# Retention queries scaled on GpSimd instead of retention outputs on VectorE, with a deeper input pipeline

## The chip, the cores and the metric

The kernel runs on one core of a Trainium2 chip. The metric is the time on the device in microseconds (us), lower is better. The engines are named as in the profile: PE is TensorE's matmul side and PEld its weight loads, DVE is VectorE, ACT is ScalarE, POOL is GpSimd, SP is the engine that issues most DMAs. 

## What is computed

Three layers, all float32, one after the other on 2304 tokens (4 batches of 576) of width 512:

```python
def _attn_ref(q, k, v):                      # q, k, v: (4, 8, 576, 64)
    scores = scale * np.matmul(q, k.transpose(0, 1, 3, 2))
    gamma = 1.0 - 2.0 ** (-5.0 - np.arange(H, dtype=np.float32))
    rel = pos[:, None] - pos[None, :]
    Dmat = np.where(rel >= 0, gamma[:, None, None] ** rel[None, :, :], 0.0)
    return np.matmul(scores * Dmat, v)       # retention
# rms norm, then (silu(x @ w_gate) * (x @ w_val)) @ w_out, d_ff = 1536
# then 8 experts: relu(x @ w1[e]) @ w2[e], weighted by a Sinkhorn-normed router
```

Only the retention layer and the first weights of the gated layer are touched by the change.

## The kernel before

The work has three stages: retention with the norm sums (about the first 87 us), the gated layer (five blocks of tokens times six sweeps over the weights), and the experts, which take most of the time. The order of the instructions on each engine is the order in which the code is written (a manual schedule); an engine runs its own list in that order, and the lists wait for each other by semaphores.

Retention runs over 16 pairs of heads, i = 0 to 15: batch b = i // 4, pair pr = i % 4, two heads in one 128-partition tile. The 576 positions are four chunks of 128 and a tail of 64. For a pair:

- `load_pair` (L279) brings kT and qT (feature by position, 128x576), ks (position by feature, 128x512) and vs (128x576); kT and ks have two buffers each, qT and vs three.
- `scale_keys` (L289) multiplies ks by a decay on ACT (L295).
- `scores` (L297): 8 matmuls of kT and qT into `sc` in PSUM (L310) and two for the tail (L313), then DVE multiplies by a mask into `am` (L314). The masks are made at the start on POOL from a causal table and the decays g_in (L460).
- `states` (L320): 8 small matmuls of ks and vs (L331), a scan over the chunks on DVE (L334) and the tail mask `mt` (L335).
- `outputs` (L338): matmuls of the states with qT for the tail (L347, L349) and the chunks (L352), then of `am` with vs (L361). DVE scales the results by the decays `g_out` while it moves them from PSUM into `acc`: the tail in L357 (128x64), the chunks in L366 (128x512). ACT squares them (L371) and, for pr > 0, POOL adds the squares to those of the batch so far (L373).

The loop at L473 writes, for pair i: the loads of pair i+2 (qT, vs) and one weight tile, `scores(i + 1)`, the first part of `outputs(i)`, `states(i + 1)`, the second part of `outputs(i)`, the loads of pair i+3 (kT, ks), `scale_keys(i + 2)`, one call of `step_weights`, and the last part of `outputs(i)`. In places it also runs the norm: `norm_sums` (L389) of batch 0, 1 and 2 starts at i = 5, 9 and 13 with five matmuls into `ss` (L398), then DVE, a power on POOL (L405) and more DVE; `norm` (L412) of batch 0 runs from i = 7, that of batch 1 from i = 13; each of the two has matmuls into `rb` (L421).

`step_weights` (L161) takes each weight tile that is being narrowed one step on. A tile of 64-bit weights (128x1024 words) becomes a float32 pair high and low in steps that go back and forth: ACT abs (L134); DVE three instructions (L136 to L138); ACT abs (L140); DVE sign (L142), which frees the raw tile; ACT cast to the high part (L156); DVE subtraction for the low part (L158). Two tiles are under way at most.

Of the kernel before, what the change touches and what calls it, by code (L numbers as in the profile page):

```python
# [9 lines left out]
F32 = mybir.dt.float32  # L10
# [7 lines left out]
B, H, S, D = 4, 8, 576, 64  # L18
NP = H // 2
# [6 lines left out]
C = 128  # L26
# [32 lines left out]
def retention_glu_experts(ctx: ExitStack, tc: tile.TileContext, a, out):  # L59
# [22 lines left out]
    const.tile([128, 40], F32, name="spacer_w")  # L82
# [183 lines left out]
    tables = tabs.tile([128, 2 * H + 2 * NP + C + TAIL], F32, name="tables")  # L266
    at, views = 0, []
    for size in (H, H, NP, NP, C, TAIL):
        views.append(tables[:, at:at + size])
        at += size  # L270
    g_in, g_key, g_step, g_tail, causal, causal_t = views
    steps = acc_d[:, :, (B - 1) * S:(B - 1) * S + D * NC]
    g_out = tabs.tile([128, NP, C], F32, name="g_out")
    mhalf = nrm.tile([128, NC + 1], F32, name="mhalf")
# [4 lines left out]
    def load_pair(i, *names, queue=nc.sync):  # L279
        if i >= B * NP:  # L280
            return
        b, pr = divmod(i, NP)
        t = {}
        for n in names:
            t[n] = ld.tile([128, a[n].shape[-1]], F32, tag=n, name=f"{n}{i}", bufs=2 if n[0] == "k" else 3)
            queue.dma_start(t[n], a[n][b, pr])
        loaded.setdefault(i, {}).update(t)

    def scale_keys(i):  # L289
        if i >= B * NP:  # L290
            return
        for h in range(2):
            hh = 2 * (i % NP) + h
            ks = loaded[i]["ks"].rearrange("p (c h d) -> p c h d", h=2, d=D)[:, :, h, :]
            nc.scalar.mul(ks, ks, g_key[:, hh:hh + 1])  # L295

# [41 lines left out]
    def outputs(i):  # L338
# [18 lines left out]
        nc.vector.tensor_mul(xf[:, NC * C:], ot, g_out[:, pr, :TAIL])  # L357
        yield
        for c in range(NC):
# [6 lines left out]
        nc.vector.tensor_mul(  # L366
            xf[:, :NC * C].rearrange("p (c i) -> p c i", c=NC), o,
            g_out[:, pr:pr + 1, :].to_broadcast([128, NC, C]),
        )
# [85 lines left out]
    nc.gpsimd.memset(wg[:, KD * E:], 0.0)  # L455
    nc.scalar.dma_start(tables, a["tables"])
    mask_rows = masks.rearrange("p a b c d -> p (a b c) d")
    for pr in range(NP):
        for hh in (2 * pr, 2 * pr + 1):
            nc.gpsimd.tensor_mul(mask_rows[:, hh, :], causal, g_in[:, hh:hh + 1].to_broadcast([128, C]))  # L460
        step = steps[:, pr].rearrange("p (d c) -> p d c", c=NC)[:, :, 1:]
        nc.gpsimd.tensor_copy(step, g_step[:, pr:pr + 1].to_broadcast([128, D, NC - 1]))
    load_pair(0, "kT", "ks")
    load_pair(0, "qT", "vs", queue=nc.scalar)
    load_pair(1, "kT", "qT")
    load_pair(1, "ks", "vs")
    nc.sync.dma_start(g_out.rearrange("p h i -> p (h i)"), a["g_out"])
# [6 lines left out]
    load_pair(2, "kT", "ks")  # L474
    for i in range(B * NP):
        b, pr = divmod(i, NP)
        load_pair(i + 2, "qT", "vs")
        load_weights(1)
# [9 lines left out]
        load_pair(i + 3, "kT", "ks")  # L488
        scale_keys(i + 2)
        step_weights(load=False, apart=1)  # L490
# [896 lines left out]
def _tables():  # L1387
# [16 lines left out]
    t["tables"] = np.concatenate(joined, 1)  # L1404
# [56 lines left out]
```

## Time and profile before

| | |
|---|---|
| median of 3 runs | 1983.78 us (1983.07 to 1984.54) |
| profiled execution | 1984.0 us, its span 1981.7 us |
| PE busy | 1964.9 us, 99% of the span |
| DVE / ACT / POOL busy | 1554.6 / 944.1 / 877.8 us |
| chain that ended last | PE 90%, DVE 5%, DMA 3%, ACT 1% |

The span is the profiled execution from its first to its last instruction; the 2.3 us beside it lie outside the instructions. A busy PE says that matmuls follow each other, not that they run at their peak, so the stretches in which PE waits, and for what, tell more than the busy share.

### The profile page before, as it was taken

What the parts mean: (1) busy time and instruction counts of PE and PEld (TensorE: products, weight loads), DVE (VectorE), ACT (ScalarE), POOL (GpSimd) and SP (SyncE); (2) the same over time, 40 slices, a digit from 0 to 9 for tenths busy, and PEclk for the clock granted to TensorE, in tenths of its full rate; (3) what the DMA queues carried; (4) which work ended last, traced back from release to release, by engine and by line L of the source; (5) the groups of instructions that cost most, each with busy time, mean ns of one, the idle gap of its engine ahead of it and who ended that gap; (6) DMA issues with size and microseconds to landing.
All of it is one profiled execution on the core that took longest, in us unless ns stands there. A gap on an engine that the chain in (4) does not pass through costs nothing.

```text
span 1981.7 us, 31851 instructions
## 1 busy us (share of the span) xinstructions
PE 1964.9 (99%) x11540; PEld 1868.2 (94%) x11540; DVE 1554.6 (78%) x2496; ACT 944.1 (48%) x1902; POOL 877.8 (44%) x817
## 2 busy tenths in 40 slices
PE   9999999999999999999999999999999999999998
PEld 7788888988889989999999999999999999999998
DVE  6868999886678776777787777777787777777777
ACT  4556555544454435444455444444455444444443
POOL 2314344444144424445564445454465454544543
PEclk9999999999999999999999999999999999999999
DMA  8418999988377887667768767677667676666763
GB/s 306 162 57 292 310 325 325 317 300 264 114 291 297 296 305 279 264 254 266 270 237 296 270 241 280 252 261 274 239 260 273 252 279 258 257 262 245 277 256 143
DMA packets 167853, 515.51 MB, mean 260 GB/s; under 512 B 17960, under 2 KB 71984, under 8 KB 150032
## 3 DMA queue, kind: packets, MB, share of 16 engines
q1 hardware_dynamic: 167024, 512.00, 71.2%
q8 instruction: 90, 1.47, 0.3%
q0 software_dynamic: 240, 0.79, 0.1%
q10 hardware_dynamic: 432, 0.70, 0.1%
q14 instruction: 67, 0.55, 0.1%
HBM read 390.40 MB, written 123.02 MB: 259 GB/s over the span
## 4 chain that ended last, share of the span: by engine, by line
PE 90%; DVE 5%; DMA 3%; ACT 1%; issue 1%; SPq 0%; POOL 0%; ACTq 0%; DVEq 0%
PE py L910 10%; PE pz L910 10%; PE px L910 10%; PE qx L1145 9%; PE qy L1145 9%; PE qz L1145 9%; PE qz L910 4%; PE gv L194 4%; PE gv L196 4%; PE gv L195 4%; PE e L1145 2%; PE pv L1145 2%; PE x L195 2%; PE x L196 2%; PE x L194 2%; PE y L195 2%
## 5 line engine op out<-in xcount | busy, mean ns | idle before, releaser
L1327 POOL TENSOR_TENSOR acc<-z,a_block 128x384 f32<-128x384 f32 x83 | 84.3, 1016 | 563.1 <-DVE z L1321 563.1
L699 POOL TENSOR_TENSOR ahead_raw<-ahead_raw 128x256 f32<-128x256 f32 x164 | 150.8, 919 | 211.1 <-DVE wslots L681 71.7
L1139 DVE TENSOR_TENSOR xlo<-acc,xhi 128x384 fp32r<-128x384 f32 x250 | 236.1, 970 | 2.8 <-ACT xhi L1135 2.7
L910 PE MATMUL py<-sx,w1s 128*128 128x384 f32 x1152 | 231.8, 335 | 0.9 <-ACT py L1247 0.6
L910 PEld LDWEIGHTS py<-sx,w1s 128*128 128x128 f32 x1152 | 202.4, 188 | 4.0 <-ACT py L1247 2.6
L1135 ACT CAST xhi<-acc 128x384 fp32r<-128x384 f32 x332 | 162.0, 513 | 91.3 <-POOL acc L1327 46.5
L910 PE MATMUL px<-xhi,w1s 128*128 128x384 f32 x640 | 189.1, 336 | 0.4 <-DVE t L220 0.4
L1156 DVE TENSOR_TENSOR acc<-acc,qz 128x384 f32<-128x384 f32 x246 | 134.8, 548 | 25.2 <-PE qz L1145 25.1
L1174 ACT COPY qz<-qy 128x384 f32<-128x384 f32 x167 | 77.4, 463 | 139.4 <-PE qy L1145 132.1
L1166 ACT COPY qy<-qx 128x384 f32<-128x384 f32 x167 | 77.4, 463 | 123.6 <-PE qx L1145 116.3
L1139 POOL TENSOR_TENSOR xlo<-fifth,xhi 128x384 fp32r<-128x384 f32 x83 | 108.4, 1307 | 38.1 <-ACT xhi L1135 38.1
L1156 DVE TENSOR_TENSOR acc<-acc,qx 128x384 f32<-128x384 f32 x123 | 67.4, 548 | 70.9 <-PE qx L1145 70.9
L910 PEld LDWEIGHTS px<-xhi,w1s 128*128 128x128 f32 x640 | 117.9, 188 | 1.1 <-DVE t L220 0.7
L910 PE MATMUL pz<-sx,w1s 128*128 128x384 f32 x576 | 115.4, 334 | 0.0
L910 PE MATMUL pz<-xhi,w1s 128*128 128x384 f32 x384 | 113.4, 335 | 0.0
L1349 POOL TENSOR_TENSOR fifth<-acc 128x384 f32<-128x384 f32 x83 | 111.2, 1339 | 0.0
L1348 POOL TENSOR_TENSOR acc<-z 128x384 f32<-128x384 f32 x83 | 109.7, 1322 | 0.0
L910 PE MATMUL px<-xlo,w1s 128*128 128x384 f32 x320 | 107.0, 334 | 0.0
L910 PEld LDWEIGHTS pz<-sx,w1s 128*128 128x128 f32 x576 | 101.3, 188 | 0.7
L1135 ACT CAST xhi<-a_block 128x384 fp32r<-128x384 f32 x84 | 43.2, 514 | 121.5 <-DVE a_block L1290 121.5
L1139 DVE TENSOR_TENSOR xlo<-z,xhi 128x384 fp32r<-128x384 f32 x84 | 88.5, 1053 | 0.0
L1329 POOL TENSOR_TENSOR acc<-acc,z 128x384 f32<-128x384 f32 x83 | 85.4, 1029 | 6.5
(409 smaller groups left out, 6085.6 us busy)
## 6 DMA issues: line engine op xcount, KB each, us to landing
w1s<-w_kept SPq DMA_DIRECT2D x85, 1792.0 KB, 7.1
w2s<-w_kept SPq DMA_DIRECT2D x42, 1024.0 KB, 6.9
w_extra<-w_kept SPq DMA_DIRECT2D x42, 768.0 KB, 7.6
w2c<-w_kept SPq DMA_DIRECT2D x42, 512.0 KB, 7.7
w2c<-w_kept SPq DMA_DIRECT2D x84, 256.0 KB, 7.9
ahead_raw<-in_w_dram SPq DMA_DIRECT2D x41, 512.0 KB, 5.4
w_kept<-w1s SPq DMA_DIRECT2D x11, 1792.0 KB, 6.6
w_kept<-wslots SPq DMA_DIRECT2D x74, 256.0 KB, 4.4
```

The costliest lines, as they stand in the source:

```text
L194: nc.tensor.matmul(ps, lhsT=lh, rhs=rh, start=start, stop=False)
L195: nc.tensor.matmul(ps, lhsT=lh, rhs=rl, start=False, stop=False)
L196: nc.tensor.matmul(ps, lhsT=ll, rhs=rh, start=False, stop=stop)
L699: nc.gpsimd.tensor_sub(w[:, o, :], w[:, x, :], w[:, y, :])
L910: nc.tensor.matmul(ps, lhsT=l, rhs=r[:, k, :], start=start and k == 0 and i == 0, stop=k == 1 and i == 2, skip_group_check=True,)
L1135: nc.scalar.copy(hi, x)
L1139: (engine or nc.vector).tensor_sub(lo, x, f32(hi))
L1145: nc.tensor.matmul(ps, lhsT=l, rhs=r, start=start and i == 0, stop=i == 2, skip_group_check=True)
L1156: nc.vector.tensor_add(dst, dst, ps)
L1329: nc.gpsimd.tensor_sub(sums[1], sums[0], z[:, 1, :])
L1348: nc.gpsimd.tensor_sub(sums[2], z[:, 1, :], z[:, 0, :])
L1349: nc.gpsimd.tensor_sub(sums[3], h_blocks[1], sums[1])
```

## The change

POOL multiplies qT by the decays in place, before the scores are made from it (`scale_queries`, for every pair but the first). The mask and the state products then come out already scaled, and the outputs are only copied from PSUM, by ACT instead of DVE; pair 0 keeps the old way. kT, ks and qT get one more buffer each, and the loads of kT, qT and ks are written one pair earlier. At the start the masks are made on DVE instead of POOL; the tables come in two pieces, the first one in a part of `acc` that is free then; g_out moves from SP's queue to ACT's. The first weight tiles are asked for from pair 2 on instead of pair 0, and `step_weights` is called twice for pairs 4, 5 and 9.

```diff
--- before.py
+++ after.py
@@ -79,7 +79,7 @@
     rms_g = const.tile([128, KD], F32, name="rms_g")
     ident = const.tile([128, 128], F32, name="ident")
     ones = const.tile([128, 128], F32, name="ones")
-    const.tile([128, 40], F32, name="spacer_w")
+    mhalf = const.tile([128, 40], F32, name="mhalf")[:, :NC + 1]
     wg = const.tile([128, KD * E + LANE - E], F32, name="wg")
     prob = const.tile([128, TT, E], F32, name="prob")
 
@@ -263,15 +263,12 @@
     psa = psa_pools.enter_context(tc.tile_pool(name="psa", bufs=2, space=PSUM))
 
     masks = tabs.tile([128, NP, 2, 1, C], F32, name="masks")
-    tables = tabs.tile([128, 2 * H + 2 * NP + C + TAIL], F32, name="tables")
-    at, views = 0, []
-    for size in (H, H, NP, NP, C, TAIL):
-        views.append(tables[:, at:at + size])
-        at += size
-    g_in, g_key, g_step, g_tail, causal, causal_t = views
+    tables = tabs.tile([128, H + NP + TAIL], F32, name="tables")
+    g_key, g_tail, causal_t = tables[:, :H], tables[:, H:H + NP], tables[:, H + NP:]
+    first_tables = acc_d[:, 0, 2 * S:2 * S + H + NP + C]
+    g_in, g_step, causal = first_tables[:, :H], first_tables[:, H:H + NP], first_tables[:, H + NP:]
     steps = acc_d[:, :, (B - 1) * S:(B - 1) * S + D * NC]
     g_out = tabs.tile([128, NP, C], F32, name="g_out")
-    mhalf = nrm.tile([128, NC + 1], F32, name="mhalf")
     block_states = [tabs.tile([128, D * NC], F32, name=f"block_states{i}") for i in range(2)]
     heads = [slice(h * D, (h + 1) * D) for h in range(2)]
     loaded, staged, squares = {}, {}, {}
@@ -282,7 +279,7 @@
         b, pr = divmod(i, NP)
         t = {}
         for n in names:
-            t[n] = ld.tile([128, a[n].shape[-1]], F32, tag=n, name=f"{n}{i}", bufs=2 if n[0] == "k" else 3)
+            t[n] = ld.tile([128, a[n].shape[-1]], F32, tag=n, name=f"{n}{i}", bufs=4 if n == "qT" else 3)
             queue.dma_start(t[n], a[n][b, pr])
         loaded.setdefault(i, {}).update(t)
 
@@ -293,6 +290,15 @@
             hh = 2 * (i % NP) + h
             ks = loaded[i]["ks"].rearrange("p (c h d) -> p c h d", h=2, d=D)[:, :, h, :]
             nc.scalar.mul(ks, ks, g_key[:, hh:hh + 1])
+
+    def scale_queries(i):
+        if i >= B * NP:
+            return
+        qt, decay = loaded[i]["qT"], g_out[:, i % NP, :]
+        by_chunk_of_q = qt[:, :NC * C].rearrange("p (c i) -> p c i", c=NC)
+        decays = decay.rearrange("p (o i) -> p o i", o=1).to_broadcast([128, NC, C])
+        nc.gpsimd.tensor_mul(by_chunk_of_q, by_chunk_of_q, decays)
+        nc.gpsimd.tensor_mul(qt[:, NC * C:], qt[:, NC * C:], decay[:, :TAIL])
 
     def scores(i):
         if i >= B * NP:
@@ -354,7 +360,10 @@
                     start=c == 1, stop=False, skip_group_check=True,
                 )
         xf = acc_d[:, pr, b * S:(b + 1) * S]
-        nc.vector.tensor_mul(xf[:, NC * C:], ot, g_out[:, pr, :TAIL])
+        if i:
+            nc.scalar.copy(xf[:, NC * C:], ot)
+        else:
+            nc.vector.tensor_mul(xf[:, NC * C:], ot, g_out[:, pr, :TAIL])
         yield
         for c in range(NC):
             for h, hs in enumerate(heads):
@@ -363,10 +372,11 @@
                     start=False, stop=c == NC - 1, skip_group_check=True,
                 )
         yield
-        nc.vector.tensor_mul(
-            xf[:, :NC * C].rearrange("p (c i) -> p c i", c=NC), o,
-            g_out[:, pr:pr + 1, :].to_broadcast([128, NC, C]),
-        )
+        xf_chunks = xf[:, :NC * C].rearrange("p (c i) -> p c i", c=NC)
+        if i:
+            nc.scalar.copy(xf_chunks, o)
+        else:
+            nc.vector.tensor_mul(xf_chunks, o, g_out[:, pr:pr + 1, :].to_broadcast([128, NC, C]))
         sq = sp.tile([128, S], F32, tag="sq", name=f"sq{i}")
         nc.scalar.activation(sq, xf, AF.Square)
         if pr:
@@ -453,29 +463,36 @@
     nc.gpsimd.memset(ones, 1.0)
     nc.gpsimd.memset(mhalf, -0.5)
     nc.gpsimd.memset(wg[:, KD * E:], 0.0)
+    load_pair(0, "kT", "ks")
+    load_pair(0, "qT", queue=nc.scalar)
+    nc.scalar.dma_start(first_tables, a["first_tables"])
     nc.scalar.dma_start(tables, a["tables"])
+    load_pair(0, "vs", queue=nc.scalar)
+    load_pair(1, "kT", "qT")
+    nc.scalar.dma_start(g_out.rearrange("p h i -> p (h i)"), a["g_out"])
+    load_pair(1, "ks", "vs")
+    load_pair(2, "kT", "qT", "ks")
     mask_rows = masks.rearrange("p a b c d -> p (a b c) d")
     for pr in range(NP):
         for hh in (2 * pr, 2 * pr + 1):
-            nc.gpsimd.tensor_mul(mask_rows[:, hh, :], causal, g_in[:, hh:hh + 1].to_broadcast([128, C]))
+            nc.vector.tensor_mul(mask_rows[:, hh, :], causal, g_in[:, hh:hh + 1].to_broadcast([128, C]))
         step = steps[:, pr].rearrange("p (d c) -> p d c", c=NC)[:, :, 1:]
         nc.gpsimd.tensor_copy(step, g_step[:, pr:pr + 1].to_broadcast([128, D, NC - 1]))
-    load_pair(0, "kT", "ks")
-    load_pair(0, "qT", "vs", queue=nc.scalar)
-    load_pair(1, "kT", "qT")
-    load_pair(1, "ks", "vs")
-    nc.sync.dma_start(g_out.rearrange("p h i -> p (h i)"), a["g_out"])
+        if not pr:
+            scale_queries(1)
     table = pad[:, 128:130].bitcast(F32)
     nc.scalar.activation(table, ones[:, :1], AF.Silu)
     scale_keys(0)
     scale_keys(1)
     scores(0)
     states(0)
-    load_pair(2, "kT", "ks")
     for i in range(B * NP):
         b, pr = divmod(i, NP)
-        load_pair(i + 2, "qT", "vs")
-        load_weights(1)
+        load_pair(i + 2, "vs")
+        load_pair(i + 3, "kT", "qT", "ks")
+        if i > 1:
+            load_weights(1)
+        scale_queries(i + 2)
         if i == 2:
             nc.sync.dma_start(rms_g, a["rms_g"])
             nc.sync.dma_start(ident, a["ident"])
@@ -485,9 +502,9 @@
         next(out_steps)
         states(i + 1)
         next(out_steps)
-        load_pair(i + 3, "kT", "ks")
         scale_keys(i + 2)
-        step_weights(load=False, apart=1)
+        for _ in range(2 if i in (4, 5, 9) else 1):
+            step_weights(load=False, apart=1)
         next(out_steps)
         if i in SUMS_AT:
             next(sums[i // NP - 1], None)
@@ -1401,7 +1418,9 @@
     joined = [np.broadcast_to(t.pop(n), (128, t_size)) for n, t_size in (
         ("g_in", H), ("g_key", H), ("g_step", NP), ("g_tail", NP), ("causal", C), ("causal_t", TAIL),
     )]
-    t["tables"] = np.concatenate(joined, 1)
+    g_in, g_key, g_step, g_tail, causal, causal_t = joined
+    t["first_tables"] = np.concatenate([g_in, g_step, causal], 1)
+    t["tables"] = np.concatenate([g_key, g_tail, causal_t], 1)
     return {k: np.ascontiguousarray(v, dtype=np.float32) for k, v in t.items()}
```

The new order shows at three places. The number in a name such as sq5 or qT8 is the pair; for raw0, cv0 it is the weight tile; ss0, rv0, ry0 belong to batch 0.

POOL, from the end of pair 3 to pair 7, before:

```order
L373 TENSOR_TENSOR sq3_446<-sq3_446,sq2_383 128x576
L373 TENSOR_TENSOR sq5_571<-sq5_571,sq4_508 128x576
L405 TENSOR_TENSOR ry0_581<-rv0_580,mhalf_114 128x5
L373 TENSOR_TENSOR sq6_648<-sq6_648,sq5_571 128x576
L373 TENSOR_TENSOR sq7_715<-sq7_715,sq6_648 128x576
```

and in the changed kernel, from the queries of pair 7 on:

```order
L300 TENSOR_TENSOR qT7_456<-qT7_456,g_out_113 128x512
L301 TENSOR_TENSOR qT7_456<-qT7_456,g_out_113 128x64
L383 TENSOR_TENSOR sq5_585<-sq5_585,sq4_519 128x576
L415 TENSOR_TENSOR ry0_595<-rv0_594,mhalf_79 128x5
L300 TENSOR_TENSOR qT8_525<-qT8_525,g_out_113 128x512
L301 TENSOR_TENSOR qT8_525<-qT8_525,g_out_113 128x64
L383 TENSOR_TENSOR sq6_662<-sq6_662,sq5_585 128x576
L300 TENSOR_TENSOR qT9_605<-qT9_605,g_out_113 128x512
```

The scaling of pair 8's queries now stands behind the square sum of pair 5 and the power of batch 0.

ACT around pair 5 (its squares are sq5), before:

```order
L371 ACTIVATE sq4_508<-acc_84 128x576
L295 ACTIVATE ks7_500<-ks7_500,tables_112 128x4x64 x2
L156 CAST wslots_85<-cv1_380 128x512
L371 ACTIVATE sq5_571<-acc_84 128x576
L295 ACTIVATE ks8_563<-ks8_563,tables_112 128x4x64 x2
```

and in the changed kernel:

```order
L381 ACTIVATE sq4_519<-acc_84 128x576
L364 COPY acc_84<-u5_462 128x64
L292 ACTIVATE ks7_458<-ks7_458,tables_112 128x4x64 x2
L156 CAST wslots_85<-cv0_446 128x512
L140 ACTIVATE cv1_512<-cv1_512 128x512
L156 CAST wslots_85<-cv1_512 128x512
L377 COPY acc_84<-o5_545 128x512
L381 ACTIVATE sq5_585<-acc_84 128x576
L364 COPY acc_84<-u6_531 128x64
```

Where one weight cast stood between the squares of pairs 4 and 5, there are now a cast, an abs, a second cast and the copy of pair 5's outputs.

DVE between the tail masks mt5 and mt6, before:

```order
L335 SCALAR_TENSOR_TENSOR mt5_487<-u5_453,tables_112 128x64
L142 SCALAR_TENSOR_TENSOR cv0_313<-raw0_200,cv0_313 128x512
L366 TENSOR_TENSOR acc_84<-o4_467,g_out_113 128x512
L314 TENSOR_TENSOR am6_518<-sc6_517,masks_111 128x1024
L357 TENSOR_TENSOR acc_84<-u5_453,g_out_113 128x64
L334 SCALAR_TENSOR_TENSOR block_states0_115<-acc_84,u6_516 128x256
L335 SCALAR_TENSOR_TENSOR mt6_550<-u6_516,tables_112 128x64
```

and in the changed kernel, as far as the first cast's subtraction:

```order
L341 SCALAR_TENSOR_TENSOR mt5_496<-u5_462,tables_112 128x64
L136 TENSOR_SCALAR cv0_446<-cv0_446 128x512
L137 TENSOR_SCALAR cv0_446<-raw0_329 128x512
L138 SCALAR_TENSOR_TENSOR cv0_446<-cv0_446 128x512
L136 TENSOR_SCALAR cv1_512<-cv1_512 128x512
L137 TENSOR_SCALAR cv1_512<-raw1_395 128x512
L138 SCALAR_TENSOR_TENSOR cv1_512<-cv1_512 128x512
L320 TENSOR_TENSOR am6_533<-sc6_532,masks_111 128x1024
L340 SCALAR_TENSOR_TENSOR block_states0_114<-acc_84,u6_531 128x256
L341 SCALAR_TENSOR_TENSOR mt6_565<-u6_531,tables_112 128x64
L142 SCALAR_TENSOR_TENSOR cv0_446<-raw0_329,cv0_446 128x512
L158 TENSOR_TENSOR wslots_85<-cv0_446,wslots_85 128x512
```

The output scalings are gone, and six narrowing instructions stand ahead of pair 6's mask where one stood.

## Rows read from the trace of the kernel before

**Rows 1.** Part 1 of the page: busy time, share of the span, instructions.

```profile
PE 1964.9 (99%) x11540; PEld 1868.2 (94%) x11540; DVE 1554.6 (78%) x2496; ACT 944.1 (48%) x1902; POOL 877.8 (44%) x817
```

**Rows 2.** Busy time by stretch: PE, PEld, DVE, ACT, POOL, granted clock, DMA share, GB/s.

```profile
9.10:25.45 16.35, 13.96 (x219) 12.30 (x217) 8.65 (x16) 6.03 (x12) 1.41 (x1) 0.90 0.90 303
25.45:61.04 35.59, 35.39 (x603) 31.22 (x601) 32.38 (x68) 19.77 (x41) 10.76 (x8) 1.00 0.88 298
61.04:87.07 26.03, 22.63 (x340) 19.27 (x338) 25.56 (x51) 13.33 (x26) 8.26 (x7) 0.93 0.52 172
87.07:180.00 92.93, 92.68 (x440) 79.19 (x440) 64.78 (x102) 53.88 (x110) 24.36 (x22) 1.00 0.39 131
```

**Rows 3.** Timeline of PE: start, duration, instruction, idle before and its releaser.

```profile
9.10 1.78 PE L310 MATMUL sc<-qT,kT 64*128 64x128 f32 x16
...
14.02 1.16 PE L310 MATMUL sc<-qT,kT 64*128 64x128 f32 x16 [0.27 <-DMA qT<-in_qT_dram]
...
20.17 1.65 PE L310 MATMUL sc<-qT,kT 64*128 64x128 f32 x16 [2.12 <-DMA qT<-in_qT_dram]
...
25.45 1.16 PE L310 MATMUL sc<-qT,kT 64*128 64x128 f32 x16
...
29.41 1.16 PE L310 MATMUL sc<-qT,kT 64*128 64x128 f32 x16
...
33.37 1.16 PE L310 MATMUL sc<-qT,kT 64*128 64x128 f32 x16
...
38.51 1.16 PE L310 MATMUL sc<-qT,kT 64*128 64x128 f32 x16
...
61.04 1.16 PE L310 MATMUL sc<-qT,kT 64*128 64x128 f32 x16
...
65.69 1.16 PE L310 MATMUL sc<-qT,kT 64*128 64x128 f32 x16 [0.63 <-DMA qT<-in_qT_dram]
...
72.35 1.16 PE L310 MATMUL sc<-qT,kT 64*128 64x128 f32 x16
...
83.37 0.45 PE L347 MATMUL u<-qT,block_states 64*64 64x64 f32 x4 [1.84 <-DVE mt L335]
...
87.08 0.50 PE L194 MATMUL gv<-xhi,wslots 128*128 128x512 f32 x1
```

**Rows 4.** Groups of 0 to 90 us, DVE: busy, mean ns, idle before.

```profile
L366 DVE TENSOR_TENSOR acc<-o,g_out 128x512 f32<-128x512 f32 x16 | 10.9, 684 | 0.0
```

**Rows 5.** The same view, ACT: copies of PSUM and the squares.

```profile
L371 ACT ACTIVATE sq<-acc 128x576 f32<-128x576 f32 x16 | 10.9, 680 | 17.4 <-DVE acc L366 12.9 <-DVE rv L402 2.8 <-DVE rt L407 1.0
...
L424 ACT COPY y<-rb 128x512 f32<-128x512 f32 x2 | 1.1, 569 | 0.0
...
L425 ACT COPY y<-rb 128x64 f32<-128x64 f32 x2 | 0.4, 216 | 0.0
```

**Rows 6.** Timeline of ACT at the start: the keys of pair 1.

```profile
9.30 0.91 ACT L295 ACTIVATE ks<-ks,tables 128x256 f32<-128x256 f32 x2 [2.61 <-DMA ks<-in_ks_dram]
```

**Rows 7.** Groups of 0 to 90 us, POOL: square sums, powers, masks.

```profile
L373 POOL TENSOR_TENSOR sq<-sq,sq 128x576 f32<-128x576 f32 x12 | 17.6, 1465 | 59.3 <-ACT sq L371 59.3
...
L405 POOL TENSOR_TENSOR ry<-rv,mhalf 128x5 f32<-128x5 f32 x3 | 3.6, 1187 | 0.0
...
L460 POOL TENSOR_TENSOR masks<-tables 128x128 f32<-128x128 f32 x8 | 3.0, 395 | 2.2 <-DMA tables<-in_tables_dram 2.2
```

**Rows 8.** The same view, two steps of narrowing a weight tile.

```profile
L142 DVE SCALAR_TENSOR_TENSOR cv<-raw,cv 128x512 int32<-128x512 int32 x6 | 4.3, 714 | 0.0
...
L156 ACT CAST wslots<-cv 128x512 fp32r<-128x512 f32 x6 | 3.7, 621 | 8.8 <-DVE cv L142 8.8
```

**Rows 9.** Timeline of DVE in pair 5: the tail mask mt6.

```profile
37.17 0.26 DVE L335 SCALAR_TENSOR_TENSOR mt<-u,tables 128x64 f32<-128x64 f32 x1
```

**Rows 10.** Timeline of POOL and DVE around 72 us.

```profile
71.49 1.40 POOL L434 TENSOR_TENSOR xlo<-acc,xhi 128x576 fp32r<-128x576 f32 x1
...
71.94 1.24 DVE L136 TENSOR_SCALAR cv<-cv 128x512 f32<-128x512 f32 x1
```

## The prediction

> **What bounds the kernel now.** I read the busy times first, then the stretches, then the timeline of PE, and last the groups of the other engines. PE is busy 99% of the span [rows 1], so time can only come from where PE waits or runs at the lower clock. The stretches show where that is: from 87.07 to 180 us PE is busy 92.68 of 92.93 us, while in the retention stage before it, 61.04 to 87.07, it has 22.63 of 26.03 us and DVE is full with 25.56 [rows 2]. From 25.45 to 61.04 PE has 35.39 of 35.59, though DVE is at 32.38 there [rows 2]: for the middle pairs PE is the bound, for the last ones DVE. So the change is worth what it does to the start of the gated layer at 87.08, and because PE hardly waits after it, I pass a shift of that point on to the end one to one.
>
> The timeline of PE gives the losses. An undisturbed pair takes 29.41 - 25.45 = 3.96 us from scores to scores, one with the five norm sums 38.51 - 33.37 = 5.14 [rows 3]. Against 3.96 the pairs lose 14.02 - 9.10: 0.96; 20.17 - 14.02: 2.19, most of it a wait of 2.12 for qT; 25.45 - 20.17: 1.32, after that wait; 65.69 - 61.04: 0.69, with 0.63 for qT; 72.35 - 65.69: 2.70; and near the end one wait of 1.84 for DVE's mt [rows 3]. That is 9.7 us in all, and the most that a better retention stage can give, nearly.
>
> The 1.32 is the clock. After the 2.12 us wait the eight-chunk scores took 1.65 where 1.16 is usual [rows 3], and the mean granted clock of the stretch is 0.90 [rows 2]: part of it ran at the lower of the two levels, 1.2 instead of 2.4 GHz.
>
> **The change, part by part.**
>
> *What leaves DVE.* 15 scalings of 128x512 at 0.68 us [rows 4] and 15 tails, sized as the like copy on ACT, 0.22 [rows 5]: 13.5 us. For the middle pairs that is worth nothing, because PE is the bound there. It counts in the late stretch, where 2.70 + 1.84 = 4.5 us stand open; DVE still has the norm and the weights there, and the ends are 0 and 4.5. I take half, -2.3.
>
> *Loads.* The first two weight tiles (2 x 0.52 MB by their shape) move behind the loads of pair 5, and one more buffer lets kT, qT and ks go out a pair earlier; SP's queue is in order, so they still stand behind vs of the pair before, which waits for a buffer of `outputs`. At some 300 GB/s [rows 2] the 1.05 MB are 3.5 us, more than any wait for qT. I let the waits for qT and the slow clock behind the first go: 2.19 + 1.32 + 0.69 = -4.2. Next to be late would be PE's own work.
>
> *The start.* The scores of pair 1 now need qT1 scaled, and that needs g_out, which ACT issues after qT0, two tables and vs0. With kT0, ks0, kT1 and qT1 this is 2.11 MB, the same bytes that went ahead of the keys of pair 1 before, and those were in at 9.30 [rows 6]. The scaling takes two POOL instructions. The nearest rows are the square sum, 1.47 for 576 columns, and the mask, 0.40 for 128 [rows 7]; the line through them gives 1.31 + 0.24 = 1.55, with 0.90 (DVE's price for the same work [rows 4, 5]) and 1.87 (a whole square sum and a mask) as ends. So pair 1 starts at 9.30 + 1.55 = 10.85 instead of 9.10: +1.75, between 0 and 2.5. Masks on DVE, the table load behind g_out's issue and ks of pair 0 I cost at nothing, as PE is busy with the scores of pair 0 meanwhile; without that cover each is below 1 us, inside these ends.
>
> *ACT's copies.* 0.57 and 0.22 per pair, the same shapes from PSUM [rows 5]; ACT is at 19.77 of 35.59 [rows 2], so its busy time is not the matter. Its order is: the copy and the squares stand behind the weight steps, and POOL's square sum behind them.
>
> *The wait that the change adds.* POOL is in order. The scaling of pair i+2 stands behind the square sum of pair i-1, and PE needs it one pair (3.96) after the outputs of pair i-1 end. In between stand: copy 0.57, squares 0.68, square sum 1.47, scaling 1.55 = 4.27 [rows 5, 7]. That is 0.3 late, for pairs 1, 2, 3, 7 and 11: +1.5, between 0 and 2. After pr = 0 there is no square sum.
>
> For pair 5 more stands in the way. `step_weights` runs twice for pairs 4 and 5, so ACT's copy of pair 5's outputs waits for a chain that goes back and forth after mt6: sign (DVE) 0.71, cast (ACT) 0.62, subtraction and sign (DVE, both priced as L142) 0.71 + 0.71, cast 0.62 [rows 8]. Then come copy 0.57, squares 0.68, square sum 1.47, the power 1.19, scaling of pair 8 1.55 [rows 5, 7]. Sum 8.83. The outputs of pair 5 ended at 38.51 - 1.18 (the norm sums, 5.14 - 3.96) = 37.33 [rows 3], and mt6 ended at 37.17 + 0.26 = 37.43 [rows 9], 0.1 later. In the new order six narrowing instructions stand ahead of it instead of one and a scaling; the four more are at most 4 x 0.71 [rows 8], at least 0, and I take 1.0, since PE gave DVE some slack. PE wants pair 8 at 5.14 after the outputs of pair 5. The wait is 0.1 + 1.0 + 8.83 - 5.14 = +4.8, between 3.1 and 6.6.
>
> For pair 9 the same happens a second time, with the power of batch 1 and pair 12: three narrowing instructions (1.5, at most 2.1), sign 0.71, cast and abs 0.62 each, then the same copy, squares, square sum, power and scaling: 8.91 - 5.14 = +3.8, between 3.1 and 4.4. For pair 13 no queries are left to scale.
>
> *The clock again.* Two waits of over 2.12 us would each bring the loss seen after that one: 2 x 1.3 = +2.6, between 0 and that.
>
> *Port.* DVE's L136 started at 71.94, took 1.24, and ended 0.29 after a POOL instruction that had begun at 71.49 and ended at 72.89 [rows 10]: it stood 0.95 for it. I leave this out of the sum and give it a rival. The Trainium skill, SBUF — State Buffer, "Who interferes with whom", states the rule: a VectorE instruction with one SBUF input, outside the two-port modes, does not contend with GpSimd; one with two SBUF inputs or in such a mode does, and whichever starts second is blocked for the whole of the other. By that rule the scalings taken away (one input in PSUM) never waited for GpSimd, while each multiplication added can hold up the narrowing and the norm; it speaks against the change, and the row agrees with it.
>
> *Sum.* 1.75 + 4.8 + 3.8 + 1.5 + 2.6 - 4.2 - 2.3 = +8.0, against the profiled execution 1984.0 us; its span 1981.7 and the 2.3 beside it stay as they are otherwise. The median of the runs, 1983.78, is 0.2 below, and from it I predict 1991.8. With all terms at their lower ends (0 + 3.1 + 3.1 + 0 + 0 - 4.2 - 4.5) it is -2.5, 1981; at their upper ends (2.5 + 6.6 + 4.4 + 2 + 2.6 - 4.2) +13.9, 1998.
>
> **The rivals.**
>
> *Relief wins (faster).* If POOL has the queries of pairs 8 and 12 ready within 5.14 us of the outputs, none of its waits is seen, and the loads and all of the late stretch are gained: 1.75 - 4.2 - 4.5 = -7, 1977. For it: POOL is busy 10.76 of 35.59 us [rows 2], so there is room. Against: it is not room but order that decides, and 8.8 would have to shrink to 5.1. Chance 0.18.
>
> *Even.* The two long chains cost half of what I sum (the casts come early, since the tiles are in long before): 1.75 + 4.3 + 0.8 - 4.2 - 2.3 = +0.4, within 0.2% of before, 1984. This is also what would be seen if the extra buffers change nothing and POOL's waits are small. Chance 0.16.
>
> *Port decides (slower still).* From pair 9 on DVE is full; one stand of 0.95 [rows 10] for each of seven pairs is 6.6, of which half on the path is 3.3, and the 2.3 of relief are lost: 8.0 + 5.6 = +13.6, 1997. It decides as soon as DVE's mask is what PE waits for, as at 83.37 [rows 3]. Chance 0.12.
>
> *The forecast,* POOL's order: 0.54, of which 0.05 lands within 0.2%.
>
> **How the numbers follow.** 0.2% is 4 us, about what a measurement of this kernel can tell from no change. Faster: the first rival, 0.18. Same: the second, and 0.05, together 0.21. Slower: 0.49 + 0.12 = 0.61. The forecast's own range is 1981 to 1998. To hold 8 in 10 the range reaches into the first rival, to 1979, where about 0.13 is left out, and takes in the port case up to 1998, where about 0.05 is.
>
> **What would show it.** Right: in the new timeline PE stands for a POOL instruction before the scores of pairs 8 and 12, some 4 to 5 us each; pair 1 starts at about 10.9; the waits for qT's load are gone; the gated layer starts near 95 us; and after it nothing differs. Each DVE scaling is missing, ACT has copies of 0.57. Wrong: no wait for POOL above 1 us before the scores, or a gated layer that starts before 83 us; or the difference lies behind the start of the gated layer, which would say that my one-to-one shift is false.

## The result, and the profile after

The changed kernel takes 1995.79 us (median of 6 runs, 1995.38 to 1998.17), the kernel before on the same chip 1983.69 (6 runs): a ratio of 1.0062, 95% interval 1.0049 to 1.0075. It is slower by 12.1 us. The prediction, 1991.8 with a range of 1979 to 1998, has the sign and holds the time; it is 4 us low. The profiled execution took 1995.38 us, 11.4 more than the one of before; its span is 1993.3.

Part 1 of the page of the changed kernel answers to [rows 1]:

```profile
PE 1966.6 (99%) x11540; PEld 1868.8 (94%) x11540; DVE 1555.5 (78%) x2474; ACT 953.8 (48%) x1932; POOL 899.3 (45%) x839
```

13.5 us of scalings left DVE, 1.9 us of masks came to it, and its busy time has not fallen (1554.6 before). The busy time by stretch, cut where the scores of pairs 1, 4 and 11 and the gated layer begin (columns as in [rows 2]):

```profile
10.73:25.47 14.74, 14.58 (x216) 12.96 (x217) 7.08 (x11) 5.12 (x13) 6.89 (x11) 0.79 0.71 236
25.47:63.49 38.02, 32.83 (x528) 28.80 (x529) 26.71 (x43) 22.65 (x51) 19.90 (x21) 0.96 0.81 280
63.49:97.60 34.11, 26.32 (x413) 22.52 (x411) 31.31 (x48) 20.41 (x45) 20.05 (x16) 0.95 0.50 158
97.60:190.00 92.40, 91.92 (x433) 78.06 (x434) 64.87 (x101) 53.63 (x109) 22.96 (x22) 1.00 0.37 127
```

PE now waits 5.2 us in the middle stretch, where before it had waited 0.2 from pair 4 to pair 12 [rows 2], and 7.8 in the late one. The timeline of PE says for whom; it answers to [rows 3]:

```profile
10.73 2.08 PE L316 MATMUL sc<-qT,kT 64*128 64x128 f32 x16 [1.52 <-POOL qT L300]
...
17.32 1.16 PE L316 MATMUL sc<-qT,kT 64*128 64x128 f32 x16
...
39.11 1.16 PE L316 MATMUL sc<-qT,kT 64*128 64x128 f32 x16
...
47.91 2.08 PE L316 MATMUL sc<-qT,kT 64*128 64x128 f32 x16 [4.77 <-POOL qT L300]
...
71.20 1.77 PE L316 MATMUL sc<-qT,kT 64*128 64x128 f32 x16 [3.68 <-POOL qT L300]
...
82.83 1.16 PE L316 MATMUL sc<-qT,kT 64*128 64x128 f32 x16 [2.29 <-POOL qT L300]
...
93.46 0.45 PE L353 MATMUL u<-qT,block_states 64*64 64x64 f32 x4 [1.46 <-DVE mt L341]
...
97.60 0.50 PE L194 MATMUL gv<-xhi,wslots 128*128 128x512 f32 x1 [0.36 <-ACT acc L377]
```

PE waits for GpSimd before pairs 1, 8, 12 and 14; the waits for the load of qT are gone. The gated layer starts at 97.60 instead of 87.08, 10.5 us later, and takes all of its lateness to the end: from its start to the end of the span it is 1895.7 us against 1894.6.

The timelines of DVE and POOL before pair 8 show both things that the change does around GpSimd (rows of the two engines, in order of start):

```profile
43.61 1.40 POOL L383 TENSOR_TENSOR sq<-sq,sq 128x576 f32<-128x576 f32 x1 [4.81 <-ACT acc L364]
...
43.79 1.77 DVE L158 TENSOR_TENSOR wslots<-cv,wslots 128x512 fp32r<-128x512 f32 x1
...
44.97 1.65 POOL L415 TENSOR_TENSOR ry<-rv,mhalf 128x5 f32<-128x5 f32 x1
46.60 1.25 POOL L300 TENSOR_TENSOR qT<-qT,g_out 128x512 f32<-128x512 f32 x1
46.65 1.23 DVE L417 TENSOR_TENSOR rt<-ry 128x5 f32<-128x5 f32 x1 [1.09 <-POOL ry L415]
47.82 0.31 POOL L301 TENSOR_TENSOR qT<-qT,g_out 128x64 f32<-128x64 f32 x1
```

The scaling of pair 8 (46.60) comes last behind a square sum (43.61) and a power (44.97): that is the order. And two DVE instructions with both inputs in SBUF, which start inside a POOL instruction, come to their end only behind it: L417, five columns that take 0.17 us elsewhere, took 1.23 and ended at 47.88, 0.03 after L300; L158, 0.68 before, took 1.77 and ended at 45.56, 0.55 after the square sum. Time that an instruction loses so is called a stand here; it is what the prediction calls the port. Even the power stood for L158: 1.65 instead of 1.19 [rows 7]. Over the whole stage the groups of DVE show it:

```profile
L440 DVE SCALAR_TENSOR_TENSOR acc<-acc,rms_g,y 128x576 f32<-128x576 f32 x5 | 6.8, 1368 | 3.3 <-ACT y L435 3.3
L158 DVE TENSOR_TENSOR wslots<-cv,wslots 128x512 fp32r<-128x512 f32 x5 | 5.2, 1045 | 0.9 <-ACT wslots L156 0.9
...
L419 DVE SCALAR_TENSOR_TENSOR ry<-rt,ry 128x5 f32<-128x5 f32 x3 | 2.9, 966 | 0.1
L417 DVE TENSOR_TENSOR rt<-ry 128x5 f32<-128x5 f32 x3 | 2.6, 869 | 1.6 <-POOL ry L415 1.6
```

Before, the means of these four were 947, 682, 167 and 154 ns. With the stands of some smaller groups it comes to some 10 us. So about three quarters of the 13.5 us that DVE was to be freed of are given back as stands.

### The profile page after: what moved, and what is told of

Read it like the earlier page. It is cut to its first block, busy times and chain, and to the rows that moved or that the text cites. A ratio compares the mean times of both kernels' runs of the same rounds, so it can differ in the third digit from the quotient of the medians.

```text
span 1993.3 us, 31901 instructions
## 1 busy us (share of the span) xinstructions
PE 1966.6 (99%) x11540; PEld 1868.8 (94%) x11540; DVE 1555.5 (78%) x2474; ACT 953.8 (48%) x1932; POOL 899.3 (45%) x839
## 4 chain that ended last, share of the span: by engine, by line
PE 88%; DVE 6%; DMA 3%; ACT 1%; issue 1%; POOL 1%; SPq 0%; DVEq 0%; ACTq 0%; POOLq 0%
PE py L927 10%; PE pz L927 10%; PE px L927 10%; PE qx L1162 9%; PE qy L1162 8%; PE qz L1162 8%; PE qz L927 4%; PE gv L194 4%; PE gv L196 4%; PE gv L195 4%; PE e L1162 2%; PE pv L1162 2%; PE x L195 2%; PE x L196 2%; PE x L194 2%; PE y L195 2%
```

## The experiments

Theory A is the prediction's: GpSimd's order. The scaling stands behind a square sum that stands behind ACT's and DVE's doubled narrowing, and PE waits. The rival, B, is the port: DVE stands for GpSimd's reads, and everything behind DVE comes late. Each run was timed against the kernel before on its own chip; the stage's end is the first matmul of the gated layer (L194) in its profile, which is one execution and lies up to 2.1 us from the median.

| run | stage ends, us | median, us | ratio to before, 95% |
|---|---|---|---|
| kernel before | 87.08 | 1983.5 to 1985.5 | |
| the change | 97.60 | 1995.79 | 1.0062 (1.0049 to 1.0075) |
| rest_only | 88.69 | 1986.88 | 1.0016 (1.0007 to 1.0025) |
| step_after_copy | 94.69 | 1993.25 | 1.0039 (1.0025 to 1.0052) |
| scale_ahead | 98.78 | 1996.63 | 1.0057 (1.0044 to 1.0070) |
| pool_reads | 89.22 | 1988.64 | 1.0022 (1.0013 to 1.0031) |
| write_only | 95.73 | 1995.78 | 1.0052 (1.0040 to 1.0064) |
| ahead_write_only | 89.01 | 1985.49 | 1.0001 (0.9993 to 1.0010) |
| rest_single | 84.11 | 1990.42 | 1.0025 (1.0016 to 1.0033) |
| single_step | 98.83 | 2003.28 | 1.0089 (1.0075 to 1.0103) |
| pair1_dve | 95.02 | 1993.49 | 1.0047 (1.0034 to 1.0059) |
| four_dve | 89.28 | 1988.61 | 1.0024 (1.0014 to 1.0034) |
| rest_early | 84.03 | 1982.53 | 0.9990 (0.9982 to 0.9999) |
| late_pool | 81.54 | 1981.19 | 0.9990 (0.9981 to 0.9999) |

From the stage's end to the end of the span every profile has 1894.6 to 1898.1 us, but for the two runs with single steps behind late weights (1903.3 and 1902.6). So what the stage loses reaches the end, to within the 3.5 us by which the profiles differ behind it; the 1.1 us that the change seems to lose there lie inside that.

**rest_only**: DVE scales all outputs again, the rest of the change stays.

```diff
-        if i:
-            nc.scalar.copy(xf_chunks, o)
-        else:
-            nc.vector.tensor_mul(xf_chunks, o, g_out[:, pr:pr + 1, :].to_broadcast([128, NC, C]))
+        nc.vector.tensor_mul(xf_chunks, o, g_out[:, pr:pr + 1, :].to_broadcast([128, NC, C]))
...
-        if not pr:
-            scale_queries(1)
...
-        scale_queries(i + 2)
```

> The changed kernel with its scaling taken back: VectorE scales all outputs again, and the loads, buffers, opening order, table pieces and doubled weight steps stay as changed. Order theory (the loss is GpSimd's in-order queue, in which the scaled queries stand behind square sums and powers): no wait for GpSimd before any scores, the waits for the query load gone too, the late VectorE stretch as in the kernel before: about 4 us below the kernel before, 1978 to 1983. Rival that the rest of the change costs (opening, doubled steps): most of the loss stays, 1990 or more. Port theory (GpSimd's reads hold up VectorE): also near 1980, so it is not told from the order theory here.

The time is that of before plus 3 us. So the scaling on GpSimd is what costs, about 9 us, but the rest gains nothing, against what A expected. All waits for qT are gone, and in their place PE waits for DVE: 0.83 us at the outputs of pair 8, 1.76 at those of pair 12, 1.80 at the end. Two later runs (rest_single and rest_early) say why.

**step_after_copy**: the second narrowing step of pairs 4, 5 and 9 moves behind the copy of the outputs.

```diff
-        for _ in range(2 if i in (4, 5, 9) else 1):
-            step_weights(load=False, apart=1)
+        step_weights(load=False, apart=1)
         next(out_steps)
+        if i in (4, 5, 9):
+            step_weights(load=False, apart=1)
```

> The changed kernel, but the second weight step of pairs 4, 5 and 9 is called behind the copies and squares of that pair instead of ahead of them; the same instructions otherwise. Order theory: ScalarE's copy of pair 5 starts some 1.3 us earlier and that of pair 9 some 3 us earlier, so the wait before the scores of pair 8 falls from 4.8 to about 3.4 and that of pair 12 from 3.7 to under 1, and one slow-clock stretch of 1.3 goes: about 1990 (1988 to 1992). Port theory: the same reads beside the same VectorE work, so within 1.5 us of the changed kernel's 1995.8.

The wait of pair 8 fell from 4.77 to 3.29 us, that of pair 12 from 3.68 to 1.32, and the copy of pair 5 came 1.38 us earlier (40.79 for 42.17): all near what A expected. But a new wait for GpSimd, of 1.88, stands before pair 13, and the time fell by 2.5 us by the medians (4.6 by the ratios) where A expected some 6.

**scale_ahead**: the scaling is written ahead of the square sum that it stood behind.

```diff
     states(0)
+    scale_queries(2)
...
-        scale_queries(i + 2)
...
             step_weights(load=False, apart=1)
+        scale_queries(i + 3)
         next(out_steps)
```

> The changed kernel, but the scaling of pair i+3's queries is written ahead of pair i's last step, so that it stands ahead of pair i's square sum and power in GpSimd's queue, as soon as its load is in; the same instructions otherwise. Order theory: the waits before pairs 8, 12 and 14 (4.8, 3.7, 2.3) fall under 1 us each and with them the two slow-clock stretches: 12 us or so come back, 1982 to 1986. Port theory: the reads are the same, so 1992 or more. Rival that the doubled steps alone hold the pairs up by way of the late copies: about half stays, 1988 to 1991.

This should have settled it for A, and it gained nothing. From pair 2 on the long waits for GpSimd are gone (the longest is 1.18), but PE now waits for DVE and ACT. Its timeline up to the outputs of pair 8, rows of DVE, POOL and PE:

```profile
47.50 1.26 POOL L300 TENSOR_TENSOR qT<-qT,g_out 128x512 f32<-128x512 f32 x1
47.55 1.24 DVE L417 TENSOR_TENSOR rt<-ry 128x5 f32<-128x5 f32 x1 [1.09 <-POOL ry L415]
...
49.00 1.39 POOL L383 TENSOR_TENSOR sq<-sq,sq 128x576 f32<-128x576 f32 x1
49.09 1.33 DVE L419 SCALAR_TENSOR_TENSOR ry<-rt,ry 128x5 f32<-128x5 f32 x1
...
50.34 1.21 DVE L320 TENSOR_TENSOR am<-sc,masks 128x1024 f32<-128x1024 f32 x1
...
52.38 0.45 PE L353 MATMUL u<-qT,block_states 64*64 64x64 f32 x4 [2.14 <-DVE mt L341]
```

GpSimd has a next instruction ready here and starts it when its power is done, 0.05 us before the DVE instruction that wants that power. L417 stands for it and L419 for the one after; the mask of pair 8, behind them, begins 2.79 us after L417, and PE waits for the tail mask that follows.

**pool_reads**: the kernel before, with two GpSimd multiplications more per pair (pairs 1 to 14) that read g_out and write a scratch tile; nobody waits for them.

```diff
+        if 0 < i < B * NP - 1:
+            pool_reads(i)
         scores(i + 1)
...
+        nc.gpsimd.tensor_mul(scratch[:, :NC * C], flat, flat)
+        nc.gpsimd.tensor_mul(scratch[:, NC * C:], flat[:, :TAIL], flat[:, :TAIL])
```

> The kernel before with two extra GpSimd multiplications per pair for pairs 1 to 14, of the shapes of the query scaling, from the decay table into a scratch tile that nobody reads: the reads and GpSimd time of the change without anybody waiting for their result. Order theory: only VectorE's stands at the shared port are added, which count in the late stretch alone: 0 to 4 us over the kernel before, 1984 to 1988. Port theory: most of the change's loss, 1992 to 1996.

1.0022: the reads alone, with nobody waiting for their result, cost some 4 us; in the profile, one of the faster runs, the stage ends 2.1 us later. DVE's L137 rose from 420 to 854 ns, L142 from 714 to 926. It is real, a little above A's range, but a third of the loss.

**write_only** and **ahead_write_only** tell the port from the order in the changed kernel itself: the scaling is left out, and GpSimd writes that read nothing stand in its place, in the change's order and in that of scale_ahead. The queries become a constant by it.

```diff
...
-        nc.gpsimd.tensor_mul(by_chunk_of_q, by_chunk_of_q, decays)
-        nc.gpsimd.tensor_mul(qt[:, NC * C:], qt[:, NC * C:], decay[:, :TAIL])
+        for at in (0, TAIL, 0):
+            nc.gpsimd.memset(qt[:, at:at + NC * C], 0.01)
```

> The changed kernel, in which the scaling of the queries is replaced by three GpSimd memsets of 128x512 with a constant over the same queries (left out: the scaling, so queries of pairs 1 to 15 become a constant). The order on every engine, the waits for qT and roughly GpSimd's time for a pair (three writes, some 1.2 to 1.8 us, against 1.60) stay; GpSimd no longer reads SBUF there. Theory A (the order alone costs the time: the scaling stands behind the square sum): the same as the change, 1994 to 1997 us, wait of pair 8 between 4 and 5 us. Theory B (part of it is the port: DVE stands for each reading GpSimd instruction): DVE's subtraction L158 falls from 1045 ns towards its 682 ns of before, the waits of pairs 8 and 12 shrink by 0.5 to 1.5 us each and the end of the stage comes earlier, 1988 to 1992 us.

> The same three writes in place of the scaling (left out: the scaling), and in the code the writes of pair i+3 stand ahead of the square sum of pair i, as in the run with the scaling written ahead. With order and port both out of the way, what is left of the change is its loads, its start and its copies on ACT. If order and port together are the cause: 1980 to 1985 us, the gated layer starts before 88 us. If only the order were: that run would have shown it already. If neither (for example the doubled narrowing steps, or ACT's copies): 1990 us or more, with PE waiting for DVE's mt or am at pairs 9 to 14 as in that run.

The three writes took 1.69 us per pair, where the two multiplications took 1.74 on average, so GpSimd was nearly as busy as with the scaling. The sums of the table by stretch from 9 to 100 us, of the change and of write_only (us; busy time of PE, PEld, DVE, ACT, POOL; then the means):

```profile
sum 91.00, PE 76.33 PEld 66.33 DVE 66.70 ACT 50.30 POOL 49.77; mean PE 19.08 PEld 16.58 DVE 16.68 ACT 12.58 POOL 12.44
```

```profile
sum 91.00, PE 77.70 PEld 67.33 DVE 59.30 ACT 51.91 POOL 46.92; mean PE 19.43 PEld 16.83 DVE 14.82 ACT 12.98 POOL 11.73
```

```profile
46.34 2.08 PE L314 MATMUL sc<-qT,kT 64*128 64x128 f32 x16 [4.62 <-POOL qT L299]
...
70.72 1.20 PE L314 MATMUL sc<-qT,kT 64*128 64x128 f32 x16 [4.03 <-POOL qT L299]
...
82.33 1.16 PE L314 MATMUL sc<-qT,kT 64*128 64x128 f32 x16 [2.32 <-POOL qT L299]
```

DVE is 7.4 us less busy, and the time is hardly lower: 1.0052 for 1.0062, with intervals that overlap. The stage ends 1.87 us earlier, and 1.94 of that stand at pair 2 already (15.38 for 17.32), as the writes need no g_out; the waits of pairs 8 and 12 are still 4.62 and 4.03, that of pair 14 still 2.32. The sign that B named failed: L158 took 1022 ns on average for 1045, as it stands for the square sums, which still read. So what these runs take away is the scaling's share of the port, not all of it.

With the scaling written ahead, the same replacement brings 1.0057 down to 1.0001, 9.8 us at the stage's end (of which 0.6 stand at pair 2), where it had brought nothing in the change's order; the time and the stage's end (89.01) lie a little above the range on record. The place at which scale_ahead lost its 2.14 us reads so in ahead_write_only, DVE and POOL (its L415 to L417 are the change's L417 to L419):

```profile
47.37 1.68 POOL L299 MEMSET qT<- 128x512 f32 x3
...
47.44 0.17 DVE L415 TENSOR_TENSOR rt<-ry 128x5 f32<-128x5 f32 x1 [1.09 <-POOL ry L413]
47.64 0.17 DVE L416 SCALAR_TENSOR_TENSOR rt<-rt,rv 128x5 f32<-128x5 f32 x1
47.84 0.17 DVE L417 SCALAR_TENSOR_TENSOR ry<-rt,ry 128x5 f32<-128x5 f32 x1
47.92 1.22 DVE L318 TENSOR_TENSOR am<-sc,masks 128x1024 f32<-128x1024 f32 x1
```

The mask begins 0.48 us after the first of them. So the four runs make a square: as in the change 1.0062, order removed 1.0057, the scaling's reads removed 1.0052, both removed 1.0001. **Each of the two causes holds the time up alone**, and only taking both away gives it back. A and B were not rivals. That the queries are a constant in two of the four brings nothing by itself, as write_only's 1.0052 says. What the reads cost depends on the order: 2.1 us at the stage's end in pool_reads, where the first DVE instruction behind each power took 0.32 us on average, and 9.2 in scale_ahead, where it took 0.88.

**rest_single** and **single_step** call the narrowing once per pair, without and with the scaling on GpSimd.

```diff
-        for _ in range(2 if i in (4, 5, 9) else 1):
-            step_weights(load=False, apart=1)
+        step_weights(load=False, apart=1)
```

> The run with all outputs scaled by DVE again and the rest of the change kept (1986.9 us) had lost the gain of its loads to waits for DVE at pairs 5 to 9 and 13. Here the narrowing is also called once per pair throughout, as before the change. If the doubled calls push work ahead of DVE's masks and that ate the gain: 1980 to 1984 us, the waits for DVE's am and mt between 36 and 50 us are gone, the gated layer starts at 83 to 86 us. If DVE simply has too much to do up to the end of the stage (the total counts, not its order): 1986 to 1988 us, the waits only move.

> The changed kernel with one call of the narrowing per pair throughout. By the sum of the prediction the chain behind the outputs of pair 5 loses the second cast and sign (about 2.7 us) and that behind pair 9 about 2.5 us, and the clock recovers at one of the two waits: 1.3 more; against it, what is not narrowed then comes later. Order and doubled calls are the cause: 1988 to 1991 us, the wait of pair 8 at 1 to 3 us. DVE's stands for GpSimd are the cause: within 2 us of the change, 1993 to 1997 us, and the wait turns up at later pairs.

By the medians both are slower for it, by 3.5 us (against rest_only) and 7.5 (against the change), by the ratios 1.8 and 5.4; for rest_single the intervals of the ratios overlap. Neither lies in a range on record. rest_single does end its stage at 84.11, but then the weights are late. PE in single_step, behind the start of the gated layer:

```profile
113.36 0.50 PE L194 MATMUL x<-ghi,wslots 128*128 128x512 f32 x1 [2.14 <-ACT wslots L156]
...
117.95 0.79 PE L196 MATMUL x<-ghi,wslots 128*128 128x512 f32 x1 [3.86 <-DVE wslots L158]
```

The doubled steps pay back what the later start of the weights owes. The same two waits, 2.14 and 3.86, stand in rest_single. In the stage itself single_step's wait of pair 8 fell to 1.22, with 2.11 behind it at pair 9 and 3.89 at pair 14.

**pair1_dve** and **four_dve** leave the queries of some pairs to the old way: pair 1, and pairs 1, 8, 12 and 14.

```diff
-        if i >= B * NP:
+        if i >= B * NP or i in (0, 1, 8, 12, 14):
...
-        if i:
+        if i not in (0, 1, 8, 12, 14):
             nc.scalar.copy(xf_chunks, o)
```

> The changed kernel, in which pair 1 also keeps the old way: its queries are not scaled on GpSimd, DVE scales its outputs. This takes the wait at the start (1.52 us for qT1, and 1.67 us of slow clock behind it) away and nothing else. If a shift at the start passes one to one to the end: 3.0 to 3.5 us faster than the change, 1992 to 1993 us. If the start is given back at pair 8 and after, because GpSimd's order and DVE's work set the time there: within 1 us of the change, 1995 to 1996.5 us, and the wait of pair 8 grows by what the start has gained.

> The changed kernel, in which pairs 1, 8, 12 and 14, those before which PE stood for GpSimd by more than 1 us, keep the old way (GpSimd leaves their queries, DVE scales their outputs); the other eleven stay with GpSimd. If the four waits are a matter of GpSimd's order alone: start 3.3, waits 4.8 + 3.8 + 2.3 and 2.6 of slow clock come back, less some stands for DVE, which has 3.6 us more to do: 1979 to 1984 us, faster than before. If behind the order DVE has too much to do (as the run with the scaling written ahead says): waits for DVE's mt or am, or for GpSimd at other pairs, take their place, 1988 to 1993 us.

pair1_dve: pair 2 starts 3.08 us earlier (14.24 for 17.32), the stage ends 2.58 earlier, and the medians are 2.3 apart (3.0 by the ratios): most of the start passes on, near the first of the two cases on record. four_dve ends its stage 8.3 us earlier and is still slower than before, as its second case said. PE's timeline has the waits at the next pairs:

```profile
44.68 1.16 PE L316 MATMUL sc<-qT,kT 64*128 64x128 f32 x16 [1.89 <-POOL qT L300]
...
46.89 0.50 PE L353 MATMUL u<-qT,block_states 64*64 64x64 f32 x4 [0.78 <-DVE mt L341]
...
68.45 2.08 PE L316 MATMUL sc<-qT,kT 64*128 64x128 f32 x16 [2.98 <-POOL qT L300]
```

**rest_early**: rest_only with the weights from pair 0 on and single steps, as before the change.

```diff
-        if i > 1:
-            load_weights(1)
+        load_weights(1)
...
-        for _ in range(2 if i in (4, 5, 9) else 1):
-            step_weights(load=False, apart=1)
+        step_weights(load=False, apart=1)
```

> The run with all outputs scaled by DVE again, with the first weights asked for from pair 0 and narrowed once per pair, as before the change. What is left of the change is one more buffer for kT, qT and ks with their loads a pair earlier, and the new start. If the buffers alone took the waits for qT away: stage ends 3 to 4 us earlier than before, weights in time, 1979 to 1982 us, faster than before. If it was the weights moved back that did it: waits for qT or kT of about 2 us are back at pairs 2 to 4, and the time is that of before within 2 us, 1983 to 1986 us.

PE waits for no qT, although the weights load as early as before. So the buffers and the earlier loads take those waits away by themselves; moving the weights back was not needed for it. The stage ends at 84.03, as that of rest_single does at 84.11, with late weights and single steps too: inside the stage it is the doubled steps that cost rest_only its gain, and they are there because the weights come late. The time is 0.1% below that of before. The profile, the slowest of this kernel's runs, doesn't show the 3 us at the end of its span, only at the stage's end.

**late_pool**: rest_early with GpSimd scaling pairs 10, 11, 13 and 14 alone, written ahead.

```diff
-        if i >= B * NP:
+        if i not in (10, 11, 13, 14):
             return
...
+        scale_queries(i + 3)
         next(out_steps)
```

> The run with DVE scaling all outputs and the first weights asked for from pair 0, in which GpSimd scales the queries of pairs 10, 11, 13 and 14 alone, ahead of the square sum of three pairs before; ACT copies the outputs of these four. They lie where DVE is what PE waits for (1.19 and 0.44 us at pair 12, 1.74 us before the last tail). If taking 4 x 0.9 us from DVE there is worth more than DVE's stands for GpSimd: the two waits shrink, the stage ends before 83 us, 1979.5 to 1981.5 us. If the stands give it back here too: 1982 to 1986 us, the waits for DVE stay and L158, L440 or the like stand at 1 us and more.

PE's waits in its late stretch:

```profile
62.68 0.45 PE L353 MATMUL u<-qT,block_states 64*64 64x64 f32 x4 [0.89 <-DVE mt L341]
...
71.89 1.68 PE L316 MATMUL sc<-qT,kT 64*128 64x128 f32 x16 [1.07 <-DVE am L320]
...
77.83 0.45 PE L353 MATMUL u<-qT,block_states 64*64 64x64 f32 x4 [0.61 <-DVE mt L341]
```

They sum to 2.6 us where rest_early had 1.19, 0.44 and 1.74, 3.4. Of the 2.5 us by which the stage ends earlier, 1.6 stand at pair 2 already (12.96 for 14.59, where the clock differed), so the relief of DVE here is about 0.9 us for four scalings, by one profile of each. It has the lowest median of all the runs, 2.3 us by the medians below the one before, 0.1% by the ratio; that it is faster than rest_early isn't shown, as their intervals are the same.

## Why the prediction was right, and where it was not

*The start, +1.75.* Pair 1 starts at 10.73 for 9.10: 1.63. Not in the sum was the clock behind it: the scores of pair 1 took 2.08 us, the stretch to pair 4 had a mean clock of 0.79, and pair 2 came another 1.67 late. pair1_dve shows it, by 3.08 us at pair 2.

*The pair-8 and pair-12 waits, +4.8 and +3.8.* Measured by the steps from scores to scores, as the prediction did: 47.91 - 39.11 = 8.80 against 3.96, so 4.84; and 71.20 - 63.49 = 7.71, so 3.75. Pieces of the chain differed and cancelled in part (the power took 1.65 for 1.19, while PE began behind 1.25 of the scaling's forecast 1.55; the copy came behind the second cast, as forecast), and these waits stand in write_only almost unchanged. The order is a cause, and its size was right.

*Ordinary waits, +1.5*: 0.16 and 0.41 are seen before pairs 4 and 6, and with small lateness elsewhere 0.8; for pair 14 see below. *Slow clock, +2.6*: the matmuls from pairs 8 and 12 to the next scores took 5.20 and 5.31 for 3.96, together 2.59, at a mean granted clock of 0.69 and 0.68. The count of two was luck in part: the wait of 2.29 before pair 14 brought no lower clock, that of 1.52 before pair 1, which the term left out, did.

*Loads, -4.2*: -4.5, by the buffers, as rest_early shows. The prediction gave the weights' move a share; the runs give it none, and it made the doubled steps necessary.

*Late relief, -2.3*: this failed. From pair 13 to 14 2.36 us were lost, 2.70 before, the wait at the end was 1.46 for 1.84, and the start of the gated layer came 0.43 later behind it: about -0.3. Two things ate it. Before pair 14 PE no longer waits for DVE, but 2.29 us for GpSimd, where the sum had 0.3 among the ordinary waits. POOL's rows say what stood in the queue:

```profile
78.20 1.80 POOL L383 TENSOR_TENSOR sq<-sq,sq 128x576 f32<-128x576 f32 x1 [3.32 <-ACT sq L381]
79.97 1.41 POOL L444 TENSOR_TENSOR xlo<-acc,xhi 128x576 fp32r<-128x576 f32 x1
81.33 1.45 POOL L300 TENSOR_TENSOR qT<-qT,g_out 128x512 f32<-128x512 f32 x1
```

The scaling of pair 14 comes behind pair 11's square sum and a subtraction of the norm (L444), which the sum didn't have. In write_only this wait is 2.32, so it is order again and not the scaling's reads. The wait at the end, 1.46 for DVE's tail mask, is gone in write_only: this part is the port, which the prediction gave as a rival and left out of the sum.

The terms now sum to 10.5, the stage's end; 8.0 was forecast. The missing 2.5 are the clock behind the start (1.7), the relief (2.0), less smaller surpluses.

*The rivals.* "Port decides" was held against "GpSimd's order" as another case with its own chance. The square of four runs says that both were true at once. Its place was right (DVE's tail mask, in scale_ahead from pair 8 on and in the change at the end), and its price of a stand, 0.95 us, was near the 0.9 to 1.2 seen. "Relief wins" failed for both reasons. *The one-to-one shift* held, to within 3.5 us, in all runs whose weights were in time, and failed in the two where they weren't, by some 7 us.

The Trainium skill, SBUF — State Buffer, "Who interferes with whom", has both halves of what the runs show: a VectorE instruction with two SBUF inputs contends with a GpSimd instruction that reads SBUF, not with one that only writes. The trace agrees: L417 of the change took 1.23 us behind a reading multiplication, and the same instruction, L415 of ahead_write_only, 0.17 under a write.

## What to carry to other kernels

Work moved from VectorE to GpSimd may be exchanged rather than freed: here some 10 us of stands for 13.5 us of scalings, and nearly half of them fell on VectorE instructions of five columns. Where two causes hold the same time up, taking either away can show nothing, so an experiment that gains nothing doesn't clear its suspect; take both away, and then each. And a load or a step that is put off is paid where the consumer needs it: follow it past the end of the stage.

## What the hardware showed unexpectedly

- The length of a stand is what is left of the GpSimd instruction, however short the VectorE instruction: five columns took 1.23 to 1.40 us in place of 0.17, each ending 0.02 to 0.03 us after the GpSimd instruction. It goes both ways: the five-column power took 1.65 for 1.19 when VectorE's L158 was first.
- Short GpSimd instructions bring short stands, and writes aren't free of them: beside three writes of 0.54 us each, 1.69 together, VectorE's L137 took 0.82 or 0.83 us for 0.42 at four places of write_only and ahead_write_only.
- VectorE's masks of the scores, with one input in PSUM, took 1216 to 1221 ns on average in every kernel here, whatever GpSimd did.
- A wait of some 2 us doesn't always bring the lower clock: the scores behind a wait of 2.29 us (82.83 in the change) took the usual 1.16 at a granted clock of 1.00, those behind 1.52 us (10.73) took 2.08 at 0.50, the lower of the two levels. PE had been busy for 9.3 us without a wait before the first; before the second it had had 0.7 us of work behind another wait of 1.29 us. So the length of the wait alone doesn't say it.
